# Matrix-vector products in row form on four column groups, half of wo's backward on VectorE, and 112 zero blocks placed anew in an attention + MLP training kernel

## The chip, the cores and the metric

One core of one Trainium2 chip. The metric is device time in microseconds (us), of the slowest core where there are several. Most executions of a kernel agree within 1.5%; a run over 1.5% above the fastest of the same kernel counts as slow and is left out of the ratios. A ratio is the mean time of one kernel's fast runs over the mean of the other's fast runs of the same rounds on the same chip, so it is not quite the ratio of the medians that are quoted.

## The reference, cut to what matters

```python
def _A_ref(x, k_cache, v_cache, wq, wo):          # 32 heads, 4 kv heads, Dh 128, window W = 4096
    q = split(x @ wq)                             # wq 1024 x 4096
    k, v = repeat(k_cache[:, :, Sk - W:]), repeat(v_cache[:, :, Sk - W:])   # Sk = 32768
    o = softmax(q @ k.T * Dh ** -0.5) @ v
    return merge(o) @ wo                          # wo 4096 x 1024
def _B_ref(x, w1, b1, w2):                        # w1 1024 x 3584, w2 3584 x 1024
    h = x @ w1 + b1
    return (h * tanh(softplus(h))) @ w2
x = A_x                                           # ONE token: 1 x 1 x 1024, bf16
x = x + _A_ref(_layernorm(x), ...); x = x + _B_ref(_layernorm(x), ...)      # layers 1, 2
x = x + _A_ref(_layernorm(x), ...); x = x + _B_ref(_layernorm(x), ...)      # layers 3, 4, same weights
# outputs: x, and the gradients of x, k_cache, v_cache, wq, wo, w1, b1, w2
```

(This is a condensed rendering.) The gradients of the two caches have the caches' shape, 4 x 32768 x 128 each, and are zero except in the last 4096 positions. The kernel writes these zeros itself, as **112 blocks of 512 KB** out of one zeroed tile. When they are written does not matter to the result.

## The kernel before: the parts that matter

Every bulk transfer, loads, gradients and zero blocks alike, is issued by SyncE, in program order, into one queue. The streamed weights pass through a ring `strm` of six buffers (`NB = 6`): a seventh load is issued only when the first buffer has been read, and everything behind it in the program waits as well. `wq`, `K`, `V` and nine of the sixteen chunks of `wo` stay on the chip; `wo`'s other seven chunks, `w1` and `w2` are streamed again in each pass.

```python
def zeros(n):
    for _ in range(min(n, len(zero_jobs))):
        nc.sync.dma_start(zero_jobs.pop(0), zt[:])

def mv(acc, k, lhsT, vec, start, stop):          # the column form
    mm(acc.col(k), lhsT, vec.to_broadcast([P, R16]), start, stop)   # 128x128 weights stationary,
                                                                    # the vector moves, 16 times over
def fwd_rows2(acc, w, c, vec, first, last):      # one chunk of wo or w2, forward
    for tt in range(2):
        for dch in range(TD):                    # TD = 8
            mv(acc, dch, w[:, tt, dch * P:(dch + 1) * P], vec[:, 2 * c + tt:2 * c + tt + 1], ...)

# attn_fwd: q = acc.cols(0, 32) after 256 mv; then, in layer 3,
for c in range(NR, min(NO, NR + NB)):            # chunks of wo that are not on the chip
    held[c] = wo_load(c)
zeros(Z["A3"])
...
order = early + late if first else late + early  # wo: layer 3 begins with the streamed chunks
x_new = x_col + yacc.cols(0, TD)

# attn_bwd: dO = g @ wo^T
for i, c in enumerate(range(NR)):
    if i < len(late):
        if late[i] not in held: held[late[i]] = wo_load(late[i])
        xpose_rows2(held[late[i]])               # both halves transposed by TensorE
    bwd_rows2(dacc, wo_kept[c], c, g_bf, ...)
    ...
if first: pre.extend(w2_load(c) for c in range(NB))
zeros(Z["A3d" if first else "A1d"])

# mlp_turn (layer 4, forward and backward over w1 in 7 blocks)
for b in range(NBK):
    zeros(Z["B4"][b])
    ws[b] = [w1_block(b, hh) for hh in range(2)]
    ...
zeros(Z["B4end"])
# w2_pass: one zero block with every second chunk from the sixth on, in layer 2's backward pass

Z = dict(A3=24, B4=[0, 0, 0, 8, 1, 2, 1], B4end=8, A3c=2, A3d=34, A1c=4, A1d=12, end=10)
```

(Comments added, cuts marked by "..."; `NR = 9`, `NO = 16`, `P = 128`.) In the trace, `w_c` and `w_b` are streamed `w1`/`w2` tiles, `wo_c` streamed `wo`, `zt` the zero tile, `x_A` and `x_B` the stream after an attention and an MLP layer, and `g_A`, `g_B` its gradient.

## Time and profile before

| | before |
|---|---|
| time, median of 2 | 480.07 us (480.0 to 480.15) |
| span of the profiled run | 473.5 us (that run took 475.52 us) |
| TensorE / VectorE / ScalarE busy | 71% / 49% / 46% |
| the data queue | 171.46 MB, 93.6% of 16 engines' span |
| mean granted TensorE clock | 0.692 |

To read it I keep a **ledger**: from the table of windows in steps of 2 us, each window's length times (1 - DMA share / 1.02) is *empty*, the rest of the span is *full* (1.02 is the share that a full queue shows). Before: 35.4 empty, 438.1 full. The full time is by this definition just the queue's busy time.

### The profile page before, as it was taken

The page shows a single profiled execution, that of the slowest core. Times are in us where ns is not written, and L with a number is a line of the kernel's source. Part 1 is how long each engine was busy: PE and PEld are TensorE (multiplying, and loading weights), DVE is VectorE, ACT ScalarE, POOL GpSimd, SP SyncE. Part 2 cuts the span into 40 slices and gives each one's busy share as a digit, 9 for nine tenths or more (in the row PEclk, how much of TensorE's full clock was granted, in tenths as well). Part 3 has the DMA queues.
Part 4 walks back from the last instruction along what each step waited for, and adds up shares of the span by engine and source line. Part 5 has one row for each costly group of instructions (what it writes and reads, how often), then busy time and mean ns, then how long its engine had stood idle before and what let it go on. Part 6 is the DMA issues. An engine that isn't in the chain of part 4 may idle for free.

```text
span 473.5 us, 14753 instructions
## 1 busy us (share of the span) xinstructions
PE 334.8 (71%) x6516; PEld 262.0 (55%) x6516; DVE 233.4 (49%) x489; ACT 217.2 (46%) x267; POOL 13.5 (3%) x58
## 2 busy tenths in 40 slices
PE   0676654697873799968994777987786665879730
PEld 0674543587563799967994667987553311222100
DVE  3123010592410477733261654553466679999950
ACT  1131100272330497844670543543064379998940
POOL 2000000000000000000000000000300300000000
PEclk9977555586765699989795655998655555655555
DMA  8999999899999969998999997999848979799998
GB/s 322 395 413 413 406 403 385 300 358 371 415 416 377 401 206 312 402 386 300 413 414 415 397 399 265 325 347 415 331 193 329 403 300 386 305 402 407 406 405 330
DMA packets 52268, 172.43 MB, mean 364 GB/s; under 512 B 5200, under 2 KB 12396, under 8 KB 51180
## 3 DMA queue, kind: packets, MB, share of 16 engines
q1 hardware_dynamic: 52064, 171.46, 93.6%
q8 instruction: 51, 0.84, 0.7%
q14 instruction: 13, 0.11, 0.1%
q0 software_dynamic: 96, 0.01, 0.0%
q10 hardware_dynamic: 44, 0.01, 0.0%
HBM read 72.89 MB, written 98.58 MB: 362 GB/s over the span
## 4 chain that ended last, share of the span: by engine, by line
PE 38%; DMA 16%; ACT 8%; DVE 8%; issue 7%; POOL 1%; DVEq 0%; SPq 0%; ACTq 0%; POOLq 0%
PE tps L176 12%; PE acc L212 11%; DMA w_c<-in_B_w_dram 7%; PE ops L212 6%; DMA wo_c<-in_A_wo_dram 6%; DVE wq L135 3%; DVE K L135 2%; PE tps L542 2%; ACT st_o L138 2%; ACT wo L138 2%; DMA out_dram<-zt 2%; PE rw L794 2%; PE d L212 1%; PE sm L212 1%; ACT w_c L543 1%
## 5 line engine op out<-in xcount | busy, mean ns | idle before, releaser
L212 PEld LDWEIGHTS <-w_c 128*128 128x128 bf16 x1120 | 37.1, 102 | 23.9 <-DMA w_c<-in_B_w_dram 18.0
L543 ACT COPY w_c<-tps 128x1024 bf16<-128x1024 bf16 x28 | 28.3, 1012 | 38.8 <-PE tps L542 22.3
L212 PEld LDWEIGHTS <-wq 128*128 128x128 bf16 x1024 | 29.4, 103 | 26.4 <-DMA wq<-in_A_wq_dram 14.4
L545 DVE CUSTOM_DVE_ANT_0 scr<-w_c,gbc 128x1024 bf16<-128x1024 bf16 x28 | 34.2, 1221 | 14.3 <-DMA w_c<-in_B_w_dram 11.3
L135 DVE CAST wo<-ops 128x512 bf16<-128x512 f32 (+2 forms) x36 | 30.9, 900 | 11.6 <-PE ops L212 10.9
L138 ACT CAST wo<-ops 128x512 bf16<-128x512 f32 (+3 forms) x38 | 28.8, 842 | 6.9 <-PE ops L212 6.7
L138 ACT COPY K<-tps 128x1024 bf16<-128x1024 bf16 x18 | 17.4, 1033 | 28.3 <-PE tps L176 28.3
L212 PE MATMUL acc<-nA_pair,wq 128*128 128x16 bf16 x512 | 15.8, 174 | 16.9 <-DMA wq<-in_A_wq_dram 13.9
L542 PE MATMUL tps<-ident_bf,w_c 128*128 128x128 bf16 x224 | 23.7, 271 | 0.0
L135 DVE COPY K<-tps 128x1024 bf16<-128x1024 bf16 x14 | 9.5, 689 | 25.3 <-PE tps L176 25.3
L212 PE MATMUL acc<-a_pair,w_c 128*128 128x16 bf16 x448 | 16.1, 173 | 8.1 <-DMA w_c<-in_B_w_dram 7.9
L138 ACT COPY w_b<-tps 128x1024 bf16<-128x1024 bf16 x20 | 19.5, 1015 | 4.6 <-PE tps L176 4.4
L212 PEld LDWEIGHTS <-wo_c 128*128 128x128 bf16 x448 | 13.3, 101 | 14.6 <-DMA wo_c<-in_A_wo_dram 13.9
L212 PEld LDWEIGHTS <-wo 128*128 128x128 bf16 x576 | 17.8, 102 | 6.4 <-DMA wo<-in_A_wo_dram 3.1
L138 ACT COPY wo_c<-tps 128x1024 bf16<-128x1024 bf16 x12 | 12.1, 1012 | 19.1 <-PE tps L176 19.1
L176 PE MATMUL tps<-ident_bf,K 128*128 128x128 bf16 x256 | 20.4, 244 | 0.2 <-ACT K L138 0.2
L176 PE MATMUL tps<-ident_bf,wo_c 128*128 128x128 bf16 x224 | 15.9, 228 | 5.1 <-DMA wo_c<-in_A_wo_dram 5.1
L241 ACT ACTIVATE lnv<-var,eps_t 128x1 f32<-128x1 f32 x4 | 1.2, 295 | 39.5 <-DVE var L238 39.5
L135 DVE COPY wo_c<-tps 128x1024 bf16<-128x1024 bf16 x16 | 10.9, 690 | 17.0 <-PE tps L176 16.1
L176 PEld LDWEIGHTS <-K 128*128 128x128 bf16 x256 | 17.8, 111 | 0.8 <-issue 0.8
L135 DVE CAST K<-ops 128x1024 bf16<-128x1024 f32 x15 | 17.8, 1222 | 0.9 <-PE ops L212 0.7
L138 ACT COPY wq<-tps 128x1024 bf16<-128x1024 bf16 x16 | 15.2, 1043 | 6.5 <-PE tps L176 6.5
(305 smaller groups left out, 700.5 us busy)
## 6 DMA issues: line engine op xcount, KB each, us to landing
out_dram<-zt SPq DMA_DIRECT2D x112, 512.0 KB, 9.6
wo_c<-in_A_wo_dram SPq DMA_DIRECT2D x28, 512.0 KB, 10.2
w_c<-in_B_w_dram SPq DMA_DIRECT2D x32, 448.0 KB, 5.6
w_c<-in_B_w_dram SPq DMA_DIRECT2D x28, 512.0 KB, 6.9
out_dram<-wo SPq DMA_DIRECT2D x18, 512.0 KB, 5.9
wq<-in_A_wq_dram SPq DMA_DIRECT2D x16, 512.0 KB, 11.7
out_dram<-K SPq DMA_DIRECT2D x8, 1024.0 KB, 8.7
out_dram<-wq SPq DMA_DIRECT2D x15, 512.0 KB, 10.8
```

What stands on the lines that cost most here:

```text
L135: nc.vector.tensor_copy(out_ap, in_ap)
L138: nc.scalar.copy(out_ap, in_ap)
L176: nc.tensor.transpose(ps[:, b, :], ap, ident_bf[:])
L212: nc.tensor.matmul(out_ap, lhsT=lhsT, rhs=rhs, start=start, stop=stop, skip_group_check=True, **kw)
L241: nc.scalar.activation(lnv[:], var[:], ACT.Ln, bias=eps_t[:, 0:1], scale=1.0)
L542: nc.tensor.transpose(ps[:, b, :], w[:, 1, b * P:(b + 1) * P], ident_bf[:])
L543: nc.scalar.copy(w[:, 1, :], ps[:].rearrange("p b c -> p (b c)"))
L545: nc.vector.tensor_tensor_reduce(out=scr[:], in0=w[:, 0, :], in1=gbc[:], scale=1.0, scalar=0.0, op0=ALU.mult, op1=ALU.add, accum_out=wg[:, ...
L794: nc.tensor.transpose(ps[:, j, :], sp[:, j, :], ident_bf[:])
```

## The change

Its intent: fewer TensorE instructions on the path, part of the transposes of `wo` given to VectorE, no long wait for `wo` in layer 3, and the zero blocks moved to fit. The row form leaves its sums in rows, so two steps follow each product: VectorE copies the rows out of the accumulator (the *evacuation*), and four small products bring them back into columns (the *selection*, `rows_sel2`). Its core:

```diff
+    def row_mm(bank, c, col, mov, start, stop):        # the row form: vector stationary, weights move
+        mm(bank[32 * c:32 * c + 32, :], col.to_broadcast([P, 32]), mov, start, stop, tile_position=(0, 32 * c))
+    def rows_y(bank, row, col, par, start, stop):
+        for half in range(2):
+            row_mm(bank, 2 * half + par, col, row[:, half * 512:half * 512 + 512], start, stop)
+    def rows_sel2(bank, out_of):                       # rows back to columns, f32
+        yr = work.tile([P, 512], FP32, name="yr", tag="kp")
+        nc.vector.tensor_copy(yr[:], bank[:])
+        for j in range(4):
+            mm(out_of(j), yr[:, j * P:(j + 1) * P], sel2[:], out_of.first and j == 0, True)
 # attn_fwd: q by row_mm into two banks, then a bf16 selection; wo:
-        order = early + late if first else late + early
+        order = early + late if first else late[0:1] + early + late[1:]
-            fwd_rows2(yacc, w, c, o_bf, i == 0, i == NO - 1)
+            for tt in range(2):
+                rows_y(yrow, w[:, tt, :], o_bf[:, 2 * c + tt:2 * c + tt + 1], tt, i == 0, i == NO - 1)
+        rows_sel2(yrow, Cols8(yps, True))
 # w2_pass: the same rows_y, rows_sel2; and no zero blocks among its loads
-            if c >= NB - 1:
-                zeros(1 if (c % zk == zk - 1) else 0)
 # mlp_turn
-        zeros(Z["B4end"])
 # mlp_bwd_w1
+        bg_zeros(Z["W1"], sv["dh_bf"])                 # the same as zeros(3), before w1's loads
 # attn_bwd: eight kept chunks as rows, and of each streamed chunk one half on VectorE
+        for dch in range(TD):
+            for q in range(4):
+                row_mm(drow, q, g_bf[:, dch:dch + 1], wo_rows[:, 4 * q:4 * q + 4, dch * P:(dch + 1) * P], ...)
+            xpose(*nat_blocks(w[:, 1, :]), "a")
+            nc.vector.tensor_tensor_reduce(out=w[:, 0, :], in0=w[:, 0, :], in1=gbc[:], ..., accum_out=wdo[:, i:i + 1])
 # wq backward: 64 row_mm in place of 256 mv, then rows_sel2
-    Z = dict(A3=24, B4=[0, 0, 0, 8, 1, 2, 1], B4end=8, A3c=2, A3d=34, A1c=4, A1d=12, end=10)
+    Z = dict(A3=16, B4=[0, 0, 0, 2, 0, 2, 6], A3c=6, A3d=18, W2=2, W1=3, A1c=2, A1d=20, end=8)
```

(`W2` is used nowhere.) Before, 111 of the 112 zero blocks had a place and one was left for the end; after, 83 have one and 29 are left for the very end.

More of the change, by code (lines that the diff above doesn't have):

```diff
@@ L103 @@
     nc.vector.memset(eps_t[:], eps)
+    sel2 = keep.tile([P, 2], FP32, name="sel2")
     neg1 = keep.tile([1, 1], FP32, name="neg1")
@@ L113 @@
     make_identity(nc, ident_f[:])
+    nc.vector.tensor_add(sel2[:], ident_f[:, 0:P:64], ident_f[:, 32:P:64])
     ZC = 2048
@@ L128, in zeros, with bg_zeros @@
             nc.sync.dma_start(zero_jobs.pop(0), zt[:])
+    gate_t = keep.tile([P, 1], BF16, name="gate_t")
+    def bg_zeros(n, after):
+        zeros(n)
     ev = [0.0, 0.0]
@@ L212, in mm, with __init__, __call__ @@
         nc.tensor.matmul(out_ap, lhsT=lhsT, rhs=rhs, start=start, stop=stop, skip_group_check=True, **kw)
+    def row_mm(bank, c, col, mov, start, stop):
[8 more added lines that the diff above has]
+            mm(out_of(j), yr[:, j * P:(j + 1) * P], sel2[:], out_of.first and j == 0, True)
+    class Cols8:
+        def __init__(self, ap, first):
+            self.ap, self.first = ap, first
+        def __call__(self, j):
+            return self.ap[:, j:j + 5:4]
     pre = []
@@ L268, in ln_bwd @@
         return g_new, g_bf
-    wq_t, wo_kept, kv = [], {}, {}
+    kv = {}
+    wq_b = keep.tile([P, TD, 2, J // 2], BF16, name="wq_b")
+    wq_t = [wq_b[:, t, hf, :] for t in range(TD) for hf in range(2)]
+    wo_b = keep.tile([P, NR, 2, D], BF16, name="wo_b")
+    wo_kept = {c: wo_b[:, c, :, :] for c in range(NR)}
+    wo_rows = wo_b[:].rearrange("p c t d -> p (c t) d")
     def load_kv(pool, nm, src):
@@ L285, in wo_load @@
         if c < NR:
-            w = keep.tile([P, 2, D], BF16, name=f"wo_{c}")
-            wo_kept[c] = w
-        else:
-            w = strm.tile([P, 2, D], BF16, name="wo_c", tag="st")
-        nc.sync.dma_start(w[:], wo_v[c])
+            w = wo_kept[c]
+        else:
+            w = strm.tile([P, 2, D], BF16, name="wo_c", tag="st")[:]
+        nc.sync.dma_start(w, wo_v[c])
         return w
@@ L379, in attn_fwd @@
                 for hf in range(2):
-                    w = keep.tile([P, J // 2], BF16, name=f"wq_{t}_{hf}")
-                    nc.sync.dma_start(w[:], wq_v[:, t, hf * (J // 2):(hf + 1) * (J // 2)])
-                    wq_t.append(w)
+                    nc.sync.dma_start(wq_t[2 * t + hf], wq_v[:, t, hf * (J // 2):(hf + 1) * (J // 2)])
             load_kv(vpool, "V", v_v)
@@ L388, in attn_fwd @@
         pad = pad_tile("q_pad")
-        acc = wide(HQ)
+        top("halves")
+        qh = halves("q")
         for t in range(TD):
-            for h in range(HQ):
-                mv(acc, h, wq_t[2 * t + h // 16][:, (h % 16) * P:(h % 16 + 1) * P], n_bf[:, t:t + 1],
-                   t == 0 and h == 0, t == TD - 1)
+            for b in range(2):
+                for c in range(NC):
+                    row_mm(qh[b], c, n_bf[:, t:t + 1], wq_t[2 * t + b][:, c * 512:c * 512 + 512], t == 0, t == TD - 1)
             if first:
@@ L396, in attn_fwd @@
                     xpose(*nat_blocks(ku.pop(0)))
-        sv["qrep"] = pad_cols(pad, acc.cols(0, HQ), scale, f"q_{lname}")
+        p_bf = keep.tile([P, WC], BF16, name=f"p_{lname}")
+        qe = [p_bf[:, 0:512], work.tile([P, 512], BF16, name="qe", tag="kp", padded_shape=[P, WC])[:]]
+        nc.scalar.activation(qe[0], qh[0][:], ACT.Copy, scale=scale)
+        nc.vector.tensor_scalar(out=qe[1], in0=qh[1][:], scalar1=scale, scalar2=None, op0=ALU.mult)
+        qsel = acc_tile(HQ)
+        for b in range(2):
+            for j in range(4):
+                mm(qsel[:, 16 * b + j:16 * b + j + 13:4], qe[b][:, j * P:(j + 1) * P], ident_bf[:, 0:P:32], b == 0 and j == 0, True)
+        sv["qrep"] = pad_cols(pad, qsel[:], 1.0, f"q_{lname}")
         held = {}
@@ L401, in attn_fwd @@
                 held[c] = wo_load(c)
-            zeros(Z["A3"])
+            bg_zeros(Z["A3"], n_bf)
             for w in wq_t:
@@ L405, in attn_fwd @@
             fill(1, ["wq"], "v")
-        top("halves")
         hv = halves("s")
@@ L426, in attn_fwd @@
         ss2 = work.tile([P, 2], FP32, name="ss2")
-        p_bf = keep.tile([P, WC], BF16, name=f"p_{lname}")
         pT = work.tile([P, TJ, P], BF16, name="pT", tag="kp")
@@ L439, in attn_fwd @@
         cols_mm(oacc, pT, kv["V"], 0)
-        cols_mm(oacc, pT, kv["V"], 1)
         ssum = work.tile([P, 1], FP32, name="ssum")
@@ L448, in attn_fwd @@
         nc.vector.reciprocal(rbc[:], sps[:, 0:32])
+        cols_mm(oacc, pT, kv["V"], 1)
         o_nat = work.tile([P, HQ], BF16, name="o_nat")
@@ L461, in attn_fwd @@
                 mm(pps[64 * e:64 * e + 64, tt, :], o_row[:, tt::2], ident_bf[0:HQ, e:HQ:2], tt == 0, tt == 1, tile_position=(0, 64 * e))
-        if not first:
-            fill(2, ["V"], "av")
         o_bf = pair_col("o", lname, HQ)
@@ L474, in attn_fwd @@
         sv["p"] = p_bf
-        yacc = wide(TD)
+        yrow = acc_tile(512)
         late, early = list(range(NR, NO)), list(range(NR))
-        order = early + late if first else late + early
+        order = early + late if first else late[0:1] + early + late[1:]
         for i, c in enumerate(order):
-            w = wo_kept[c] if c < NR else (held.pop(c) if c in held else wo_load(c))
-            fwd_rows2(yacc, w, c, o_bf, i == 0, i == NO - 1)
+            if c not in held and c not in early:
+                held[c] = wo_load(c)
+            w = wo_kept[c] if c < NR else held.pop(c)
+            for tt in range(2):
+                rows_y(yrow, w[:, tt, :], o_bf[:, 2 * c + tt:2 * c + tt + 1], tt, i == 0, i == NO - 1)
+            if not first and i == 0:
+                held[NO - 1] = wo_load(NO - 1)
             if not first:
@@ L483, in attn_fwd @@
                     xq["wo"].extend(w[:, tt, :] for tt in range(2))
+        yps = sm_tile(P, TD)
+        rows_sel2(yrow, Cols8(yps, True))
         x_new = keep.tile([P, TD], FP32, name=f"x_{lname}")
-        nc.vector.tensor_add(x_new[:], x_col[:], yacc.cols(0, TD))
+        nc.vector.tensor_add(x_new[:], x_col[:], yps[:])
         return x_new, sv
@@ L522, in bcast_row, with w2_pass @@
         return big
-    def w2_pass(a_bf, g_bf, x_col, xname, wgname, zk):
-        gbc = bcast_row(g_bf)
+    def w2_pass(a_bf, g_bf, x_col, xname, wgname, gbc):
         acc = wide(TD + NW2)
+        yrow = sm_tile(P, 512)
         wg = keep.tile([P, NW2, 2], FP32, name=wgname)
@@ L532, in bwd1 @@
             for dch in range(TD):
-                mv(acc, TD + c, w[:, 1, dch * P:(dch + 1) * P], g_bf[:, dch:dch + 1], False, dch == TD - 1)
+                mv(acc, TD + c, w[:, 1, dch * P:(dch + 1) * P], g_bf[:, dch:dch + 1], c == 0 and dch == 0, dch == TD - 1)
         for c in range(NW2):
-            if c >= NB - 1:
-                zeros(1 if (c % zk == zk - 1) else 0)
             w = pre.pop(0) if pre else w2_load(c)
-            fwd_rows2(acc, w, c, a_bf, c == 0, c == NW2 - 1)
+            for tt in range(2):
+                rows_y(yrow, w[:, tt, :], a_bf[:, 2 * c + tt:2 * c + tt + 1], tt, c == 0, c == NW2 - 1)
             ps = psum1([P, 8, P], BF16, "tps")
@@ L550, in w2_pass @@
         bwd1(held.pop(), NW2 - 1)
+        rows_sel2(yrow, Cols8(acc.cols(0, TD), False))
         x_new = keep.tile([P, TD], FP32, name=xname)
@@ L570, in mlp_fwd @@
         dact = keep.tile([P, TF], FP32, name=f"dact_{lname}")
+        gbc = bcast_row(g_bf)
         m = mish_exp(hacc.cols(0, TF), TF)
@@ L576, in mlp_fwd @@
         sv["dact"] = dact
-        x_new, wg = w2_pass(a_bf, g_bf, x_col, f"x_{lname}", "wg4", 99)
+        x_new, wg = w2_pass(a_bf, g_bf, x_col, f"x_{lname}", "wg4", gbc)
         return x_new, sv, wg
@@ L610, in M, with lo0 @@
                        b == 0 and t == 0 and f == 0, b == NBK - 1 and f == FB - 1)
+        def lo0(b):
+            return max(b - 1, 0) * FB
         def X(b, hh):
@@ L617, in mlp_turn @@
         for b in range(NBK):
-            zeros(Z["B4"][b])
+            bg_zeros(Z["B4"][b], dh_bf[:, lo0(b):])
             ws[b] = [w1_block(b, hh) for hh in range(2)]
@@ L685, in attn_bwd @@
             held[c] = wo_load(c)
-        zeros(Z["A3c" if first else "A1c"])
+        bg_zeros(Z["A3c" if first else "A1c"], g_bf)
         late = list(range(NR, NO))
-        prev = None
-        for i, c in enumerate(range(NR)):
-            if i < len(late):
-                if late[i] not in held:
-                    held[late[i]] = wo_load(late[i])
-                xpose_rows2(held[late[i]])
-            bwd_rows2(dacc, wo_kept[c], c, g_bf, started=i > 0)
-            if prev is not None:
-                bwd_rows2(dacc, held.pop(prev), prev, g_bf)
-            prev = late[i] if i < len(late) else None
+        gbc = bcast_row(g_bf)
@@ new lines, in attn_bwd, with T @@
+        drow = sm_tile(P, 512)
+        wdo = work.tile([P, NO - NR], FP32, name="wdo")
+        bwd_rows2(dacc, wo_kept[NR - 1], NR - 1, g_bf, started=False)
+        for dch in range(TD):
+            for q in range(4):
+                row_mm(drow, q, g_bf[:, dch:dch + 1], wo_rows[:, 4 * q:4 * q + 4, dch * P:(dch + 1) * P], dch == 0, dch == TD - 1)
+        de = work.tile([P, 512], BF16, name="de", tag="kp", padded_shape=[P, WC])
+        nc.scalar.copy(de[:], drow[:])
+        def T(i):
+            c = late[i]
+            if c not in held:
+                held[c] = wo_load(c)
+            w = held[c]
+            xpose(*nat_blocks(w[:, 1, :]), "a")
+            nc.vector.tensor_tensor_reduce(out=w[:, 0, :], in0=w[:, 0, :], in1=gbc[:], scale=1.0, scalar=0.0,
+                                           op0=ALU.mult, op1=ALU.add, accum_out=wdo[:, i:i + 1])
@@ new lines, in M @@
+        def M(i, _):
+            c = late[i]
+            w = held.pop(c)
+            for dch in range(TD):
+                mv(dacc, 2 * c + 1, w[:, 1, dch * P:(dch + 1) * P], g_bf[:, dch:dch + 1], False, dch == TD - 1)
+            if i == 0:
+                for j in range(4):
+                    mm(dacc.cols(j, 16)[:, 0:13:4], de[:, j * P:(j + 1) * P], ident_bf[:, 0:P:32], False, True)
+            if first and i in (1, 3, 5):
+                fill(1, ["V", "K", "wq"], "a")
+        pipe(list(range(len(late))), T, M)
@@ L698, in attn_bwd @@
         if first:
             pre.extend(w2_load(c) for c in range(NB))
-        zeros(Z["A3d" if first else "A1d"])
-        if first:
+            bg_zeros(Z["A3d"], g_bf)
             fill(100, ["V"])
+        else:
+            zeros(Z["A1d"])
         do_p = work.tile([P, 2, NO], BF16, name="do_p")
-        nc.vector.tensor_copy(do_p[:], dacc.cols(0, HQ).rearrange("p (c t) -> p t c", t=2))
+        dcols = dacc.cols(0, HQ).rearrange("p (c t) -> p t c", t=2)
+        nc.vector.tensor_copy(do_p[:, 0, NR:], wdo[:])
@@ L706, in attn_bwd @@
+        nc.vector.tensor_copy(do_p[:, 0, 0:NR], dcols[:, 0, 0:NR])
+        nc.vector.tensor_copy(do_p[:, 1, :], dcols[:, 1, :])
         if first:
@@ L761, in attn_bwd @@
             run(2)
-        nacc = wide(TD)
-        for t in range(TD):
-            for h in range(HQ):
-                mv(nacc, t, wq_t[2 * t + h // 16][:, (h % 16) * P:(h % 16 + 1) * P], dq_bf[:, h:h + 1],
-                   t == 0 and h == 0, h == HQ - 1)
-            if not first:
+        nrow = acc_tile(512)
+        for h in range(HQ):
+            for half in range(2):
+                row_mm(nrow, 2 * half + h % 2, dq_bf[:, h:h + 1],
+                       wq_b[:, 4 * half:4 * half + 4, h // 16, (h % 16) * P:(h % 16 + 1) * P], h < 2, h >= HQ - 2)
+            if not first and h % 8 == 7:
                 run(1)
-        return ln_bwd(nacc.cols(0, TD), sv["n32"], sv["rstd"], g_col, lname, nxt)
+        nps = sm_tile(P, TD)
+        rows_sel2(nrow, Cols8(nps, True))
+        return ln_bwd(nps[:], sv["n32"], sv["rstd"], g_col, lname, nxt)
     def col_out(cols, n, out_flat):
@@ L929, in after_v @@
             nc.gpsimd.memset(s[:], 0.0)
-        slots.extend(wo_kept[c][:].rearrange("p t d -> p (t d)") for c in range(NR))
+        slots.extend(wo_kept[c].rearrange("p t d -> p (t d)") for c in range(NR))
         slots.extend(rp.tile([P, 2048], BF16, name=f"so{i}")[:] for i in range(2))
@@ L980 @@
     g2, g2b = attn_bwd(g3, g3b, "A3", sA3, True, "B2")
-    x4, wg2 = w2_pass(sB4["a_bf"], g2b, x3, "x_B4", "wg2", 2)
+    x4, wg2 = w2_pass(sB4["a_bf"], g2b, x3, "x_B4", "wg2", bcast_row(g2b))
     dh_of(wg2, "B2", sB2)
@@ L1020 @@
     run(1000)
-    slots.extend(w[:] for w in wq_t)
+    slots.extend(wq_t)
     dw_tall("wo", HQ, out_5.rearrange("(c p t) d -> c p t d", p=P, t=2))
```

## The prediction

> **What bounds the kernel now.** I read the page first (busy shares, 40 slices, queues), then the table of windows by stage, then the SyncE queue's timeline (every bulk transfer is issued there, in program order), then the TensorE timeline and the waits.
>
> ```profile
> span 473.5 us, 14753 instructions
> PE 334.8 (71%) x6516; PEld 262.0 (55%) x6516; DVE 233.4 (49%) x489; ACT 217.2 (46%) x267; POOL 13.5 (3%) x58
> PEclk9977555586765699989795655998655555655555
> GB/s 322 395 413 413 406 403 385 300 358 371 415 416 377 401 206 312 402 386 300 413 414 415 397 399 265 325 347 415 331 193 329 403 300 386 305 402 407 406 405 330
> q1 hardware_dynamic: 52064, 171.46, 93.6%
> q8 instruction: 51, 0.84, 0.7%
> ```
>
> No engine is near 100%; the one transfer queue is, at 93.6%. When it is full it moves some 400 to 418 GB/s, so the time is that of 172 MB plus the moments when the queue is empty. Those moments stand in the table of windows (columns: window, length, busy time of PE, PEld, DVE, ACT, POOL, clock, DMA share, GB/s):
>
> ```profile
> 88.00:97.00 9.00, 7.80 (x179) 7.36 (x180) 7.63 (x15) 4.75 (x5) 0.00 (x0) 0.70 0.68 237
> 166.00:177.00 11.00, 11.00 (x273) 11.00 (x271) 8.46 (x33) 9.98 (x14) 0.00 (x0) 1.00 0.61 199
> 232.00:257.00 25.00, 20.77 (x461) 20.49 (x459) 9.16 (x14) 12.29 (x13) 0.00 (x0) 0.77 1.03 414
> 288.00:299.00 11.00, 9.20 (x172) 8.90 (x169) 5.61 (x14) 4.21 (x5) 0.90 (x2) 0.69 0.70 223
> 340.00:348.00 8.00, 6.58 (x163) 5.00 (x161) 3.04 (x6) 3.31 (x7) 0.00 (x0) 0.50 0.15 56
> 348.00:364.00 16.00, 14.04 (x280) 8.70 (x276) 10.67 (x20) 9.31 (x18) 0.00 (x0) 0.50 0.78 307
> 376.00:400.00 24.00, 14.37 (x76) 2.80 (x74) 19.08 (x24) 20.18 (x26) 0.00 (x0) 0.50 0.88 348
> ```
>
> A full queue shows 1.02. Length x (1 - share/1.02), summed over all stages: 3.0 at 88, 4.4 at 166, 3.5 at 288, 6.8 + 3.8 at 340 to 364, 3.3 + 3.0 at 376 to 410, about 8 elsewhere: **36 us empty, 438 us full**. The change removes no bytes to speak of, so only those 36 us can be won: the floor is near 440.
>
> The timelines show where the queue serves zeros (the 112 zero blocks of 512 KB, 1.27 us each at 413 GB/s) while TensorE waits, and what the two forms of product cost:
>
> ```profile
> 110.83 27.31 SPq L128 DMA_DIRECT2D out_dram<-zt  x24
> 219.99 43.36 SPq L128 DMA_DIRECT2D out_dram<-zt  x35
> ```
>
> ```profile
> 37.34 1.91 PE L212 MATMUL s<-K,q_pad 128*32 128x512 bf16 x32
> 149.75 0.60 PE L212 MATMUL acc<-o_pair,wo_c 128*128 128x16 bf16 x16 [8.40 <-DMA wo_c<-in_A_wo_dram]
> 231.50 14.35 PE L176 MATMUL tps<-ident_bf,wq 128*128 128x128 bf16 x208
> 249.19 3.50 PE L212 MATMUL acc<-dq_pair,wq 128*128 128x16 bf16 x128 [1.05 <-issue]
> 255.66 1.13 PE L212 MATMUL acc<-dq_pair,wq 128*128 128x16 bf16 x36 [2.97 <-issue]
> 332.45 3.52 PE L212 MATMUL d<-V,do_pad 128*32 128x512 bf16 x32 [0.35 <-ACT do_pad L344]
> ```
>
> The column form takes 3.50/128 = 27 ns for one 128x128 block at clock 0.5, so 0.44 us for 16 blocks; at clock 1.0 the dh products (x32 in 0.80 us start to start) give 25 ns, 0.40 us. The four-group row form already exists here, in the scores: 32 instructions, 8 packs of 16 blocks, 1.91 us at clock 1.0 (0.24 a pack) and 3.52 us at 0.5 (0.44 a pack). **At the half clock a pack gains nothing; at the full clock it saves 0.16 us.** It always has a quarter of the instructions.
>
> **What the Trainium skill says.** "TensorEngine Tiling (Array Packing)", Key Properties: tiles work independently and can load and multiply in parallel; the 1.91 us for 32 instructions of 512 columns agrees (60 ns each). The same page, PSUM Bottleneck: tiling does not speed the evacuation; so it is here, a 128x512 f32 read costs VectorE 0.69 us, and each row product adds one. "TensorE: Matmul & The Clock Gate", Part 1: the default is the half clock and sustained activity releases it; PEclk of 5 and 9 and the 0.44 and 0.24 agree, though column products 6.6 us long (at 113) did not release it. "DMA: Bandwidth & Descriptors", Queues, rings and completion order: descriptors are consumed in ring order; the 8.40 us wait for a wo chunk queued behind 24 zeros agrees.
>
> **The change, part by part.**
> 1. *First two layers.* To 88 us the queue is full, so faster products there are worth nothing. In the first w2 pass the broadcast of g moves ahead of the activation: VectorE's stream of 14 reductions (1.26 us each) starts at 88.4 in place of 90.3, minus 1.9; the row sum's evacuation and four small products put back 0.6. Net -1.3.
> 2. *Layer 3 forward.* q: 256 products took 8.7 us to 121.65 (1.6 of it an issue wait); 16 packs, half cold, are 5.4, evacuation and selection add 1.3: -2. Two V transposes leave the chain before o (134.4 to 138.3): -3.8. The scores start warm and the reciprocal moves beside the second half of p.V: -1.4. Then wo: 18 us, 8.4 of them behind zeros. With 16 zeros instead of 24 (-10.2 us in the queue) the last chunk lands near 137.3 and the 15 others are done by then. x leaves at 139.5 instead of 156.5: **-17** with part 1.
> 3. *Layer 4 turn.* Bound by TensorE (5.2 us a block, transposes mostly), unchanged. Its queue has 10 zeros in place of 20 and stays empty about 6 us, like the 5 now.
> 4. *Layer 3 backward.* The 3.5 us wait for wo at 202 goes. The wo products took 14.1 us; now ScalarE evacuates 7 late transposes and 3 fills (10 x 1.02) behind about 5 us of broadcast, kept chunk and 8 packs: about as long. From g to dO -2.6 in all. The 14.35 us of wq transposes stay: ScalarE and VectorE evacuate them alternately, 1.04 us for two. wq's products, 11.1 us with 4.0 of issue waits (they fall before and after a group of just 128 products), become 16 warm packs, 3.9, plus 1.5 for the selection: -5.7. So the w2 pass starts near 235 instead of 261: **-26**.
> 5. *w2 and w1 passes.* With no zeros among the loads, 14 x 1.3 us on VectorE and 16 x 1.14 on TensorE: the w1 stage ends near 277 instead of 314: **-37**.
> 6. *Layer 1 backward.* VectorE's 7 reductions bound it: 12 us for 16. The last product has 4 output jobs among its packs instead of 8. Gradients done near 320 instead of 363: **-43**.
> 7. *Tail.* It gets 26 zeros (29 left over in place of 1, 8 up front in place of 10: 33 us) and 4 output jobs (5 us).
>
> **The sum, by two roads.** By path: before, the tail from 363 took 110.5 us, 103 of them full. After: 103 + 33 + 5 = 141 full, about 9 empty, from 320: a span of 470. By the ledger: empty 2 at the start, 1.5 at 88, 6 in layer 4, **13 in layer 3 backward** (18 zeros, 23 us, are issued near 200, but the next buffer comes free only with the second w2 chunk, near 238), 1 to 3 in the passes, 1 in layer 1, 9 in the tail: 34 of 36, a span of 472. The 43 us won on the path are almost exactly the 38 us of transfers moved off it. Times run 6.6 us above the span: 477 to 478.5. I put **474.5 us**, some 3 below: clock and issue waits err towards faster compute, and a backlog from the 20 late zeros may fill the tail's empty moments, which I counted in full.
>
> **Rivals.** *The queue stays the bound and the holes only move* (my main reading): for it, 93.6% and the unchanged bytes; 474 to 480. *The holes really close*: the 10.6 us at 340 to 364 are covered by 20 zeros and the tail's 6 us by its backlog, and the hole in layer 3 backward is half what I think, because w2's loads trail later; 462 to 469. Against it: the 14.35 us of wq transposes stand between the zeros and the w2 pass. *VectorE becomes the bound*: reductions of 1.26 us replace transposes in both wo backward stages and selections wait behind them; every us of compute before the tail then is a hole; 481 to 486. Against it: VectorE is 49% busy and the stages concerned have slack on TensorE.
>
> **Range and chances.** Each 1 us of hole is 1 us of time. The hole in layer 3 backward is uncertain by 3 to 5, the tail by 4, the path by 4: together about 7, tilted down. 464 to 482. 2% faster is 470.5: it needs the second rival, 0.30. Slower by 2% would need 10 us of new holes: 0.04. Within 2%: 0.66.
>
> **What would show it.** After: TensorE matmuls down by about 1800 to some 4700; issue waits gone from the wq products; layer 3's wo without a long wait; DMA share far under 1 for some 13 us between dO and the w2 pass of layer 3 backward; the 340 to 364 hole gone; VectorE's last work near 418 and some 50 us of pure zero writing at the end. I am wrong if that middle hole is missing (then faster), if the gradients are done later than 330 (then slower), or if the full queue's rate differs from 400 to 418 GB/s.

## The result, and the profile after

| | before | after |
|---|---|---|
| time, median of 2 | 480.07 us | 495.87 us (494.69, 497.05) |
| ratio | | 1.033 [1.022, 1.044]: **slower** |
| span profiled | 473.5 us | 492.8 us |
| ledger: empty / full | 35.4 / 438.1 | **57.2 / 435.6** |

The same kernel, run again later against the kernel before (e9 below), gave 1.039. From the page of the kernel after (totals, granted clock and transfer rate in 40 slices of 12.3 us, the data queue):

```profile
span 492.8 us, 11162 instructions
PE 323.9 (66%) x4700; PEld 212.3 (43%) x4700; DVE 248.3 (50%) x521; ACT 219.5 (45%) x268; POOL 13.4 (3%) x58
...
GB/s 331 389 414 412 406 323 347 332 373 377 414 320 202 255 401 188 387 407 416 153 195 402 282 340 304 418 408 288 296 319 342 307 417 403 414 411 410 420 420 333
...
q1 hardware_dynamic: 52064, 171.46, 89.6%
```

The bytes are the same to the last digit, the full rate is the same (400 to 420), matmuls fell from 6516 to 4700. Yet the queue is busy for a smaller share: 22 us more of emptiness, and only 2.5 us less of full time. The table of windows of the kernel after shows where (columns as in the prediction: window, length, busy time of PE, PEld, DVE, ACT, POOL, clock, DMA share, GB/s):

```profile
70.00:78.00 8.00, 3.88 (x101) 3.30 (x101) 1.63 (x7) 0.50 (x2) 0.00 (x0) 0.50 0.61 199
152.00:164.00 12.00, 12.00 (x291) 12.00 (x289) 9.31 (x41) 10.98 (x15) 0.00 (x0) 1.00 0.42 119
184.00:200.00 16.00, 11.66 (x238) 11.15 (x242) 7.85 (x28) 8.64 (x10) 0.00 (x0) 0.89 0.66 219
236.00:256.00 20.00, 16.33 (x242) 10.91 (x240) 13.18 (x26) 8.62 (x10) 0.00 (x0) 0.91 0.37 126
332.00:342.00 10.00, 7.73 (x67) 2.28 (x64) 5.75 (x9) 4.39 (x8) 0.00 (x0) 0.67 0.61 250
352.00:376.00 24.00, 16.35 (x67) 3.66 (x67) 18.69 (x37) 18.30 (x29) 1.07 (x6) 0.56 0.68 271
```

Read the last number but one, the DMA share: 0.42 at 152 is a queue that works less than half the time while TensorE is busy for every one of 12.00 us. These are not stalls of the engines; they are engines at work while no transfer has been given to the queue. Against that stands the end. SyncE's timeline of the kernel after (start, length, what is issued):

```profile
212.02 19.10 SPq L130 DMA_DIRECT2D out_dram<-zt  x18
250.07 9.00 SPq L331 DMA_DIRECT2D w_c<-in_B_w_dram  x8
...
447.86 37.65 SPq L130 DMA_DIRECT2D out_dram<-zt  x29
```

29 zero blocks go out from 448 us on, 37.65 us long; VectorE's last work ends at 441.4. In the first two lines, 18 zero blocks are issued from 212 on (23 us of work, behind six loads of w2) and the next load comes at 250: the 12.6 us hole between 236 and 256.

The path, read from the timelines of VectorE (the last write of each layer's x or g), in us:

| stage | before | after | difference | predicted difference |
|---|---|---|---|---|
| layers 1 and 2 forward | 110.4 | 113.6 | +3.2 | -1.3 |
| layer 3 forward | 46.2 | 29.6 | -16.6 | -15.7 |
| layer 4, both directions | 44.1 | 52.9 | **+8.8** | 0 |
| layer 3 backward | 58.0 | 48.7 | -9.3 | -9 |
| w2 pass and w1 stage | 56.9 | 50.3 | -6.6 | **-11** |
| layer 1 backward | 49.0 | 50.3 | +1.3 | **-6** |
| to the gradients of x | 364.6 | 345.4 | -19.2 | -43 |
| the tail | 108.9 | 147.4 | +38.5 | about +40 |

(The predicted differences are those between the running totals in the prediction: -17, -26, -37, -43.) The tail was foreseen; the path lost more than half of its gain.

### The profile page after: what moved, and what is told of

Same layout as the page of the kernel before. It is cut to its first block, busy times and chain, and to the rows that moved or that the text cites. A ratio compares the mean times of both kernels' runs of the same rounds, so it can differ in the third digit from the quotient of the medians.

```text
span 492.8 us, 11162 instructions
## 1 busy us (share of the span) xinstructions
PE 323.9 (66%) x4700; PEld 212.3 (43%) x4700; DVE 248.3 (50%) x521; ACT 219.5 (45%) x268; POOL 13.4 (3%) x58
## 5 line engine op out<-in xcount | busy, mean ns | idle before, releaser
L143 DVE CAST wo_b<-ops 128x512 bf16<-128x512 f32 (+3 forms) x40 | 33.1, 876 | 8.5 <-PE ops L220 8.2
L146 ACT CAST wo_b<-ops 128x512 bf16<-128x512 f32 (+2 forms) x34 | 27.0, 870 | 15.7 <-PE ops L220 15.7
L146 ACT COPY K<-tps 128x1024 bf16<-128x1024 bf16 x19 | 18.6, 1030 | 27.1 <-PE tps L184 27.1
L220 PEld LDWEIGHTS <-w_c 128*128 128x128 bf16 x672 | 22.4, 100 | 15.9 <-DMA w_c<-in_B_w_dram 10.6
L220 PE MATMUL q<-wq_b,nA_pair 128*32 128x512 bf16 x128 | 12.7, 490 | 16.6 <-DMA wq_b<-in_A_wq_dram 15.2
L754 DVE CUSTOM_DVE_ANT_0 wo_c<-wo_c,gbc 128x1024 bf16<-128x1024 bf16 x14 | 16.3, 1217 | 8.7 <-DMA wo_c<-in_A_wo_dram 6.6
L184 PE MATMUL tps<-ident_bf,K 128*128 128x128 bf16 x256 | 19.2, 232 | 0.2 <-ACT K L146 0.2
L220 PE MATMUL ops<-Tw 2*128 2x512 bf16 x56 | 15.4, 545 | 5.9 <-ACT wo_b L146 4.1
L146 ACT CAST K<-ops 128x1024 bf16<-128x1024 f32 x17 | 17.0, 1012 | 2.0 <-PE ops L220 1.4
L184 PE MATMUL tps<-ident_bf,wq_b 128*128 128x128 bf16 x256 | 17.7, 237 | 0.0
L146 ACT COPY wq_b<-tps 128x1024 bf16<-128x1024 bf16 x16 | 15.2, 1046 | 5.3 <-PE tps L184 5.3
L184 PEld LDWEIGHTS <-wq_b 128*128 128x128 bf16 x256 | 16.9, 108 | 0.4 <-issue 0.4
```

The lines of the kernel that those rows point to most:

```text
L143: nc.vector.tensor_copy(out_ap, in_ap)
L146: nc.scalar.copy(out_ap, in_ap)
L184: nc.tensor.transpose(ps[:, b, :], ap, ident_bf[:])
L220: nc.tensor.matmul(out_ap, lhsT=lhsT, rhs=rhs, start=start, stop=stop, skip_group_check=True, **kw)
L754: nc.vector.tensor_tensor_reduce(out=w[:, 0, :], in0=w[:, 0, :], in1=gbc[:], scale=1.0, scalar=0.0, op0=ALU.mult, op1=ALU.add, accum_out=w ...
```

## The experiments

Theory: the time follows the ledger, full time is constant, and the loss is the two new holes (236 to 256 and layer 4) plus the unfilled ones that the 29 late blocks no longer cover. Rivals: the new products cost time themselves; or the new placement of zeros does, whatever the products.

**The two halves of the change, each alone.** *e1_zeros_before*: the new products with the old placement.

```diff
-    Z = dict(A3=16, B4=[0, 0, 0, 2, 0, 2, 6], A3c=6, A3d=18, W2=2, W1=3, A1c=2, A1d=20, end=8)
+    Z = dict(A3=24, B4=[0, 0, 0, 8, 1, 2, 1], B4end=8, A3c=2, A3d=34, A1c=4, A1d=12, end=10)
+        zeros(Z["B4end"])            # after the last block of layer 4, as before
+            if xname == "x_B4" and c >= NB - 1 and c % 2 == 1: zeros(1)     # in the w2 pass, as before
-        bg_zeros(Z["W1"], sv["dh_bf"])
```

> The changed products with the zero blocks where the kernel before had them (24 in layer 3 forward, 12 + 8 in layer 4, 2 + 34 in layer 3 backward, 5 in the w2 pass, 4 + 12 in layer 1 backward, 10 + 1 in the tail). Theory 'holes' (time = about 438 us of full transfer queue plus its empty moments, and the new placing of zeros makes the moments): 470 to 482 us, empty moments at or under the 36 us of before. Rival 'products' (the row form, its selections and the VectorE reductions lengthen the path by themselves): 488 us or more.

*e2_products_before*: the old products with the new placement (the `Z` of after, no `B4end`, no blocks in the w2 pass, 3 before the w1 stage).

> The kernel before with the new placing of the zero blocks, its products unchanged. Theory 'holes': 26 zeros (33 us) move behind the gradients, which become ready only some 15 to 20 us earlier for the waits behind zeros that go: 488 to 500 us. Rival 'products': the placing is harmless, 472 to 482 us.

Measured, on one chip with e3 and e4 (before there: median 478.46): e1 485.3 us, ratio 1.015 [1.009, 1.022]; e2 503.3 us, 1.054 [1.050, 1.058]. e2 is as the theory had it. e1 falls between what the two theories expected and decides for neither: both halves lose time, the placement more. Its own trace shows why the new products don't pay with the old placement, in TensorE's timeline of e1 (start, length, operation, and in brackets the wait before it):

```profile
277.40 0.62 PE L220 MATMUL sm<-w_c,a_pair 128*32 128x512 bf16 x4 [12.28 <-DMA w_c<-in_B_w_dram]
```

The faster products arrive at the w2 pass while the queue is still writing 34 zero blocks, and wait 12.28 us. e1's x gradients are done at 370.5, 6 us later than before. Ledger: 45.1 empty, 437.9 full; e2: 63.3 and 438.9.

**The holes, one by one.** *e3_fill_hole*: ten of the 29 late blocks into the hole of layer 3's backward.

```diff
-    Z = dict(A3=16, B4=[0, 0, 0, 2, 0, 2, 6], A3c=6, A3d=18, ...)
+    Z = dict(A3=16, B4=[0, 0, 0, 2, 0, 2, 6], A3c=6, A3d=28, ...)
```

> The changed kernel with 28 zeros in place of 18 behind dO of layer 3 backward, so 10 fewer at the very end. Theory 'holes': they run in the 12.6 us in which the queue is empty at 236 to 252, the w2 pass starts as before: about 12 us less, 481 to 485 us, gradients at the same moment (341). Rival 'zeros hold up the path' (instruction fetches and w2's loads queue behind them): w2 pass and gradients later by several us, 489 us or more.

Measured: 483.6 us (6 runs), ratio 1.010 [1.005, 1.015]. As expected: against the kernel after's 1.033 and 1.039, some 11 to 14 us for a change of one number. The same window of e3:

```profile
236.00:256.00 20.00, 16.44 (x234) 11.33 (x232) 12.60 (x25) 8.33 (x10) 0.00 (x0) 0.83 0.96 373
```

0.96 in place of 0.37, TensorE no less busy (16.44 against 16.33). Ledger 44.3 and 439.1. So a us of hole filled was about a us of time. The gradients were not at the same moment, as expected, but 3.1 us later (348.5): layers 1 and 2 had ended 4.4 us later in this run, before any of the ten blocks. The w2 pass behind them was 4.0 us longer than in the kernel after (27.2 for 23.2), but as long (27.1) in e4, which has only 18 blocks there; so no delay by the ten blocks is seen.

*e4_block6*: the six blocks ahead of layer 4's last block of w1 go to the fourth block, where before had its eight.

```diff
-    Z = dict(A3=16, B4=[0, 0, 0, 2, 0, 2, 6], ...)
+    Z = dict(A3=16, B4=[0, 0, 0, 8, 0, 2, 0], ...)
```

> The changed kernel with the 6 zeros ahead of layer 4's last w1 block moved to the fourth block's (8, 0, 2, 0 in place of 2, 0, 2, 6). Theory: these 6 held back the last block's load and an instruction fetch (2.3 + 1.2 us issue, 3 us waits for the load, then the half clock), some 8 us of path, and at the fourth block they run in an empty moment: layer 4 about 46 us long in place of 54, 486 to 490 us in all. Rival: the stall in layer 4 has another cause (the slow small packets of these loads) and stays: 494 us or more.

Measured: 491.8 us (488.15 to 493.65), ratio 1.029. A partial miss: the kernel after stood at 1.033 and 1.039 beside its own runs of before, a gain of 2 to 5 us at most, less than expected, and the 95% intervals overlap (e4 1.023 to 1.035, the kernel after 1.022 to 1.044 and 1.031 to 1.047), so by the time alone it is not shown. In the trace layer 4 is shorter, 47.8 in place of 52.9, but the gradients are only 3.0 us earlier (342.4): part was given back behind it.

**The products.** *e5_wo_column_first*: `wo` in layer 1 in the column form again, without evacuation and selection.

```diff
-        yrow = acc_tile(512)
+        yrow = wide(TD) if first else acc_tile(512)
+            if first: fwd_rows2(yrow, w, c, o_bf, i == 0, i == NO - 1)
+            else:     ... rows_y as before ...
+        y8 = yrow.cols(0, TD) if first else yps[:]     # yps from rows_sel2
```

> The changed kernel with one part undone: layer 1's wo product in the column form again. Theory: the row form's evacuation (0.69 + 0.9 us) and its four f32 selections at the half clock (1.84 us) delay the first w1 product by 2.8 us; with six buffers full the queue stands empty 3.2 us at 70 to 78. Undone: that moment goes, x of layer 1 at about 67 (69.7 in the changed kernel), 2.5 to 4 us less in all, 491 to 494. Rival: the moment comes from the loads of w1 themselves and stays: 495 to 497.

*e8_select_bf16*: the selections in bf16 instead of f32, in every layer.

```diff
-    sel2 = keep.tile([P, 2], FP32, name="sel2")
-        yr = work.tile([P, 512], FP32, name="yr", tag="kp")
+    sel2 = keep.tile([P, 2], BF16, name="sel2")
+        yr = work.tile([P, 512], BF16, name="yr", tag="kp", padded_shape=[P, WC])
```

> The changed kernel with the row sums evacuated and selected in bf16 in place of f32, a cheaper selection everywhere. Theory: eight f32 passes (1.03 us at the full clock, 1.84 at the half) become four bf16 products (0.3 to 0.5), six times on the path: empty moment at 70 to 78 down from 3.2 to 1.5 to 2, 3 to 6 us less in all, 490 to 493. Rival: selections are not what sets the path, within 1 us of 495.9.

Measured, on one chip with e6 and e7 (before there: 476.01): e5 487.9 us, median of its three fast runs (482.88 to 489.76; a fourth, 493.06, was slow), ratio 1.021 [1.013, 1.029]; e8 486.6 us, 1.021 [1.014, 1.027]. Both gained more than expected. Look at the chain from layer 1 to layer 2, in the timelines of VectorE and TensorE of the kernel after:

```profile
67.01 0.69 DVE L235 COPY yr<-acc 128x512 f32<-128x512 f32 x1 [15.50 <-PE acc L220]
67.85 1.84 PE L220 MATMUL sm<-sel,yr 128*128 128x2 f32 x8 [0.89 <-DVE yr L235]
```

and of e8's TensorE:

```profile
67.91 0.27 PE L220 MATMUL sm<-sel,yr 128*128 128x2 bf16 x4 [0.80 <-DVE yr L235]
```

and the table of windows of e5:

```profile
70.00:78.00 8.00, 4.30 (x123) 3.66 (x120) 0.51 (x1) 0.00 (x0) 0.00 (x0) 0.50 0.99 361
```

The row form puts 0.69 us of evacuation and 1.84 us of f32 selection (eight passes for four products, at the half clock) between the last product and x. In bf16 the same selection is 0.27 us. The same window of the kernel before was as full as e5's:

```profile
70.00:78.00 8.00, 4.06 (x115) 3.42 (x111) 0.00 (x0) 0.00 (x0) 0.00 (x0) 0.50 0.99 364
```

In the kernel after x is 2.7 us later, so w1's first buffers come free later, and a queue that was full before now has a hole of 3.2 us at 70 to 78. In e5 it is gone (share 0.99 against 0.61), in e8 1.5 us of it is left. That mechanism is shown. The profiled runs (e5's is its fastest) gained more than this hole: layer 1 backward was 2.2 and 3.2 us shorter than in the kernel after, and layer 4, with the same placement of zeros, 5.2 and 3.2 us (47.8 and 49.8 long); layer 4 is taken up under *e9*.

*e9_change_again*: the kernel after, unchanged, on the chip of e10 to e12 (before there: 476.46).

> The changed kernel itself once more, on one chip with the three below, for its spread (it had two runs, 494.7 and 497.1). 488 to 497 us, 3% over the kernel before; full queue 437 us and 50 to 57 empty. If it comes near 488, part of the gains of e5 and e8 is the chip's.

Measured: 494.9 us, ratio 1.039 [1.031, 1.047], as expected. The ratio to the kernel before was 1.033 and 1.039 on two chips, and e9's interval lies clear of e5's and e8's, so their gains are hardly the chip's. Its trace separates two waits in layer 4. In the first run of the kernel after, TensorE's timeline has

```profile
175.54 0.79 PE L184 MATMUL tps<-ident_bf,wo_b 128*128 128x128 bf16 x11 [2.32 <-issue]
...
185.84 0.56 PE L220 MATMUL sm<-nB_pair,w_b 128*128 128x16 bf16 x16 [2.06 <-DMA w_b<-in_B_w_dram]
```

and in e9

```profile
183.46 0.59 PE L220 MATMUL sm<-nB_pair,w_b 128*128 128x16 bf16 x16 [3.87 <-DMA w_b<-in_B_w_dram]
```

The wait for the last block's load, behind its six zeros, is in both: 3.0 us in all in the first, 4.8 in the second. It follows the placement: e2, with the products of before and these six zeros, has 4.4 us of it, and in e1, e4, e6 and e12, where the six zeros are elsewhere, no DMA wait is left in that layer. The issue waits (3.5 us in all; time in which TensorE waited for nothing that the profile shows) are only in the first; e9's layer 4 has none and is 50.5 long. They vary from run to run, and they do not need the new placement: e1, with the old one, has 6.7 us of them, and its layer 4 took 52.3 us. Whether the new products bring more of them is not settled: the profiled runs with the new ones show 0 to 6.7 us, the fast runs with the products of before 0 to 0.8, e7's slow one 5.1.

**Zeros laid where the holes are.** The experiments above say that both halves must fit each other. *e6_laid*: e5, with the zero blocks laid into the empty moments that the kernel after showed.

```diff
-    Z = dict(A3=16, B4=[0, 0, 0, 2, 0, 2, 6], A3c=6, A3d=18, W1=3, A1c=2, A1d=20, end=8)
+    Z = dict(A3=16, B4=[1, 0, 0, 6, 2, 2, 2], A3c=6, A3d=26, W1=3, A1c=4, A1d=23, end=17)
```

> e5 with the zeros laid where the changed kernel's queue stood empty: layer 4 (1, 0, 0, 6, 2, 2, 2), 26 behind dO of layer 3, 4 and 23 in layer 1 backward, 17 before the tail, 4 at the very end. Theory 'holes' (437 us full + empty): about 23 to 28 us empty, 460 to 468 us, faster than the kernel before. Rival: zeros placed there hold up loads and fetches, each us filled is lost again on the path: 475 us or more.

*e7_before_laid*: the same kind of re-laying for the kernel before, from its own holes.

```diff
-    Z = dict(A3=24, B4=[0, 0, 0, 8, 1, 2, 1], B4end=8, A3c=2, A3d=34, A1c=4, A1d=12, end=10)
+    Z = dict(A3=18, B4=[0, 0, 0, 8, 3, 2, 1], B4end=4, A3c=3, A3d=30, A1c=4, A1d=22, end=15)
-    x4, wg2 = w2_pass(sB4["a_bf"], g2b, x3, "x_B4", "wg2", 2)
+    x4, wg2 = w2_pass(sB4["a_bf"], g2b, x3, "x_B4", "wg2", 6)
```

> The kernel before, its products unchanged, with its zeros laid anew by the same reasoning (18 in layer 3 forward in place of 24, 30 in place of 34 behind dO, 22 in place of 12 in layer 1 backward, 15 in place of 10 before the tail). Theory 'holes': the 10.6 us empty at 340 to 364 and the tail's 6 are filled, 462 to 470 us. Rival: without the row form the path is too long for it, 474 us or more, and what e6 wins is the row form's.

Measured: e6 459.8 us, ratio 0.963 [0.958, 0.968], slightly better than expected, and on the same chip 28 us under e5, from which it differs by the placement alone; e7 470.7 us, median of its three fast runs, 0.985 [0.978, 0.993], slightly worse than expected. (e7's profile fell on its slow run, 475.3 us.) Ledger of e6: 22.4 empty, 437.0 full.

*e12_before_zeros6* asks whether e6's gain is its placement alone: the products of before with e6's placement.

> The kernel before, its products unchanged, with exactly the zeros of e6. Theory: zeros and products interact; the column products' longer path (some 15 to 20 us to the gradients) leaves the same zeros in other places: 35 to 45 us empty, 472 to 482 us, against e6's 460. Rival: the placing alone is the gain, 458 to 464.

Measured: 477.9 us, ratio 1.001 [0.994, 1.008], as expected; 39.3 empty, 438.6 full. e6's placement is worth nothing to the old products.

*e10_laid_bf16*: e6 with the bf16 selections of e8 and `A3d=29`.

> e6 with bf16 selections and 29 in place of 26 zeros behind dO of layer 3. Theory: empty 18 to 22 us in place of 22.4, 454 to 459 us. Rival: the last zeros collide with w2's loads and give the gain back, 460 to 463.

Measured: **452.2 us**, ratio 0.949 [0.942, 0.956], better than expected, and 5% faster than the kernel before. From its page, and from its SyncE timeline:

```profile
span 452.9 us, 11486 instructions
...
q1 hardware_dynamic: 52064, 171.46, 97.4%
```

```profile
202.11 33.34 SPq L130 DMA_DIRECT2D out_dram<-zt  x29
239.29 13.17 SPq L331 DMA_DIRECT2D w_c<-in_B_w_dram  x8
```

29 blocks now stand where the kernel after had 18, and the next loads come at 239 instead of 250. Ledger: 17.4 empty, 435.5 full. The outputs of every kernel here agreed with the reference.

*e11_wo_back_undone*: e10 with the backward of `wo` as in the kernel before: all chunks in the column form, both halves of the streamed ones transposed, nothing of it on VectorE.

```diff
-        (broadcast, rows of the kept chunks, one half of each streamed chunk on VectorE)
+        for i, c in enumerate(range(NR)):
+            if i < len(late):
+                if late[i] not in held: held[late[i]] = wo_load(late[i])
+                xpose_rows2(held[late[i]])
+            bwd_rows2(dacc, wo_kept[c], c, g_bf, started=i > 0)
+            if prev is not None: bwd_rows2(dacc, held.pop(prev), prev, g_bf)
+            prev = late[i] if i < len(late) else None
```

> e10 with one more part undone: wo backward as before (all chunks transposed, all products in the column form, nothing on VectorE). Theory: the streaming saves some 3 us in layer 3 backward (18.8 against 15.6 from g to dO) and nothing in layer 1 backward (15.0 both), so undone costs 2 to 5 us of empty queue: 457 to 463. Rival: the part is worth nothing where the queue is covered by zeros, within 1.5 us of e10.

Measured: 452.9 us, ratio 0.950 [0.943, 0.956]; the rival is right. In this placement this part of the change is worth nothing that four runs of each could tell (16.1 empty, 434.4 full), at 12254 instructions in place of 11486.

The whole of it in one table (median us):

| zeros placed as | products of before | products of after |
|---|---|---|
| before | 480.07 (476.0 to 478.5 beside the experiments) | 485.3 (e1) |
| after | 503.3 (e2) | 495.9, 494.9 (e9) |
| e6 | 477.9 (e12) | 459.8 (e6, wo of layer 1 in columns), 452.2 (e10, also bf16 selections, three more zeros) |
| relaid for the products of before | 470.7 (e7) | not run |

And the ledger of the main ones, in us:

| | before | after | e1 | e2 | e3 | e6 | e10 | e11 | e12 |
|---|---|---|---|---|---|---|---|---|---|
| empty | 35.4 | 57.2 | 45.1 | 63.3 | 44.3 | 22.4 | 17.4 | 16.1 | 39.3 |
| full | 438.1 | 435.6 | 437.9 | 438.9 | 439.1 | 437.0 | 435.5 | 434.4 | 438.6 |

From 450 to 502 us of span, the full time stays within 434 to 439 (441.3 in e7's slow run). **The time is the empty time plus nearly a constant**, whatever the products.

## Why the prediction was right or wrong

**Right: the bound.** The queue decides, its bytes and its full rate did not change, and the ledger accounts for every kernel (the row of full times above). The floor of "near 440" was not reached, but nothing contradicts it: e10's and e11's spans are 452.9 and 450.5, with 434 to 436 of them full.

**Right: layer 3.** Forward -16.6 for -15.7. The 8.40 us wait for `wo` is gone; TensorE's timeline of the kernel after has

```profile
140.81 0.40 PE L220 MATMUL acc<-wo_c,o_pair 128*32 128x512 bf16 x4 [0.63 <-DMA wo_c<-in_A_wo_dram]
...
237.49 3.64 PE L220 MATMUL acc<-wq_b,dq_pair 128*32 128x512 bf16 x64
```

and the second line shows wq's sixteen packs in 3.64 us without an issue wait, for the 3.9 predicted. Backward -9.3 for -9, and the hole before the w2 pass is 12.6 us for the 13 predicted. e3 shows that this hole alone cost some 11 us or more.

**Right by luck in part: the tail.** 147.4 us for about 150, but its two terms missed in opposite directions: 134 full and 13 empty against 141 and 9. By the ledger the tail of before, from 364.6, was 100 full, not 103, and it grew by 34, the 33 of the 26 zeros and hardly anything for the output jobs (5 predicted).

**Wrong: the sum of holes, 34 us; it was 57.** Term by term:

| hole | predicted | measured |
|---|---|---|
| start | 2 | 2.2 |
| 70 to 78 | 0 | **3.2** |
| first w2 pass | 1.5 | 2.3 |
| layer 3 forward, 138 to 142 | 0 | 1.5 |
| layer 4 | 6 | **12.7** |
| layer 3 backward | 13 | 12.6 |
| passes | 1 to 3 | 3.1 |
| layer 1 backward | 1 | **6.3** |
| tail | 9 | **13.2** |

About the same appears on the path: it won 19.2 us where 43 were predicted, while the tail grew by 38.5. The gradients came at 345 in place of 320. The prediction had named this as a sign of "slower" (later than 330), but gave slower by 2% only 4 chances in 100. The failed step is thus the length of the path to the gradients, and by the table above its missing 24 us are 8.8 in layer 4, 7.3 in layer 1 backward, 4.5 in the first two layers and 4.4 in the w2 and w1 passes, less 1.2 by which layer 3 did better:

*Step 1, "To 88 us the queue is full, so faster products there are worth nothing."* True, but it asked only what a gain would be worth. The row form made layer 1's end 2.7 us later (evacuation 0.69, selection 1.84), and with a ring of six buffers that opened a hole. A full queue makes gains worthless, not losses. e5 and e8 show it. Nor did layer 2 get shorter by the 1.3 us: it took 43.9 in place of 43.5.

*Step 3, layer 4 "unchanged".* It was 52.9 us in place of 44.1. The step counted the blocks of zeros in this layer (ten for twenty) but not where they stood: six now came just ahead of the last block's loads and made TensorE wait 3.0 us (4.8 in e9, 4.4 in e2). Issue waits, 3.5 us in this run and none in e9 and before, are the second part, and not the placement's (e1). The third is TensorE's own busy time, which grew by 2.4 (43.6 to 45.9): right behind these waits the granted clock was 0.62 at 187 to 189 and 0.52 at 189 to 191, where before had 1.00 from 163 to the layer's end. No run keeps the clock up, so this last is argued. So the layer had ten blocks fewer to fill a time 9 us longer, and its hole came to 12.7 us in place of 6.

*Step 5, "With no zeros among the loads ... the w1 stage ends near 277 instead of 314".* For both the prediction had -11; measured, the w2 pass gave -8.8 and the w1 stage was not faster but slower by 2.2. Two lines say why. The first transposes of that stage before, and after:

```profile
291.73 3.17 PE L176 MATMUL tps<-ident_bf,w_c 128*128 128x128 bf16 x28
```

```profile
270.87 3.17 PE L184 MATMUL tps<-ident_bf,w_c 128*128 128x128 bf16 x28 [1.86 <-DMA w_c<-in_B_w_dram]
```

Before, w1's loads were in the ring already; after, three zeros (`W1=3`) go ahead of them and cost 1.86 us at the start. (e2, with the products of before and the same three zeros, waits 1.94 us there and its stage takes 27.4; e1, with the new products and no zeros there, takes 25.7.) From there to the last product TensorE takes some 22 us in both: it was bound by TensorE before as well (21.76 of 24.90 us busy), so there was little among its loads to win (1.6 us of waits for them). The prediction took its 16 x 1.14 us for a gain without asking how long the stage was before.

*Step 6, layer 1 backward -6; it was +1.3.* "12 us for 16" did not come: from g to dO the time stayed 15.0. What VectorE's reductions saved, the broadcast of g ahead of them (a 1.99 us wait of TensorE for its operand) and the row packs of the kept chunks (3.30 us, where layer 3's took 1.91) used up. The second saving came: wq's products with the output jobs among them, evacuation and selection took 14.0 us in place of 15.4, of which the products alone are 6.8 against 8.2 (three groups of 1.90, at a granted clock of 0.50 to 0.52, and one of 1.05, at 1.00, against eight of 1.02). But the way from dO to these products was 2.8 us longer, 1.03 of it an issue wait and 1.2 in a group of four output products that took 2.37 us in place of 1.18; no run tells why.

*A smaller slip:* "Times run 6.6 us above the span". The profiled run of before was a faster one, 475.52 us, so the difference is 2.0 us (1.9 after). The 6.6 pushed the estimate up, towards what came; it was wrong all the same.

**The rivals.** "The holes only move" was the right mechanism with a hole sum 23 us too small. "VectorE becomes the bound" is not what happened: e11 takes the reductions of `wo`'s backward away again and changes nothing (in e10's placement). "The holes really close" did not come from this change, but that it can is what e6 and e10 show.

**What stays open.** Whether the issue waits of up to 2.32 us come from the fetching of instructions: they come and go between runs of one kernel, and no run takes the fetching away. Why the waits in layer 4 vary under one placement: they sum to 3.5 us in e5 and 4.0 in e8 against 6.4 in the first run, which covers 2.9 of the 5.2 and 2.4 of the 3.2 us by which these layers were shorter; the rest is TensorE's busy time (43.5 and 45.0 against 45.9, at a mean granted clock of 0.96 and 0.93 against 0.90). The products of the kernel after itself were not run with e6's placement, only e5's and e8's. And e7 was one attempt at a placement, e10 the second for its products, so the 18 us between them are not all the products'.

**Its signs.** Matmuls came down to 4700 as said, and the middle hole stood where it was expected. The 340 to 364 hole moved and did not go: 4.0 us between 332 and 342, and 8.0 more between 352 and 376. VectorE ended at 441.4 instead of 418, late by the same 23 us.

## What to carry to other kernels

Where one in-order queue is the bound, keep a ledger of its empty moments and judge every change by it: shortening the compute between transfers pays only if work that can wait (here zero blocks) is laid anew into the moments that remain, and moving that work to the end just adds it to the time. Judge products and placement together: here each half alone lost (1.5% and 5.4%), both as they came lost 3.3 to 3.9%, and both fitted to each other won 5% (e10, with layer 1's `wo` in columns again and bf16 selections). And a new form of product must be charged for what follows it (evacuation, selection) at the clock of the stage in which it stands, also where the queue is full.

## What the Trainium skill lacked or had wrong

- "TensorE: Matmul & The Clock Gate", Part 1, has some 3.4 us of sustained activity release the clock. Here the kind of activity seems to count: 241 products of the column form, 6.59 us busy of 6.59, stayed at 0.50, while the row form reached a mean of 0.69 within 5.23 us. Over the same products the four profiled runs with the products of before show 0.50 to 0.52, the ten with the row form 0.56 to 0.72; no run tells what in the form does it. Windows of the kernel before, then of the kernel after, both over layer 3's q:

```profile
112.93:119.52 6.59, 6.59 (x241) 6.52 (x242) 0.13 (x1) 0.00 (x0) 0.00 (x0) 0.50 1.01 394
```

```profile
115.97:121.20 5.23, 5.22 (x64) 1.95 (x64) 0.14 (x1) 0.17 (x1) 0.00 (x0) 0.69 0.99 397
```

- The same page has no figure for small f32 products with a 128x128 stationary: four of them with two moving columns (eight instructions in the trace) took 1.84 us at the half clock and 1.03 at the full one; in bf16, 0.27 at the half clock.
- The same page, Part 3, gives a measured speedup of packing by columns alone for three groups, none for four; here four groups with 512 columns ran at 1.91 us for 32 instructions (60 ns each) at the full clock, and about 0.44 us for a pack of 16 blocks at the half clock, where the column form needs the same 0.44.
- "Runtime: NRT & Kernel Launch", Instruction fetch mechanics, calls the fetching of instructions mostly hidden. TensorE shows issue waits of 2.32 us here (2.97 before), with 37 and 51 packets on the instruction queue and the data queue mostly full. That they are fetches is a guess; that they exist and vary from run to run (3.5 us in layer 4, none in e9) is measured.
